# Two edits to a three-stage attention and MLP kernel: where a transposition is done, and how weights come back for a second batch

## The chip, the cores and the metric

The kernel runs on one core of a Trainium2 chip. A core has TensorE (PE in the profile; its weight loads are PEld), VectorE (DVE), ScalarE (ACT), GpSimd (POOL) and SyncE (SP), which here issues the DMAs; 16 DMA engines move the data. The metric is the device time of one execution in microseconds. Before the change the median of 3 runs is 804.38 us (803.98 to 806.12).

## The reference

Inputs are q, k and v, each 2 batches x 8 heads x 768 positions x 64, a 64 x 6 projection, and two pairs of weights, 512 x 2048 and 2048 x 512, in double precision.

```
bits   = (q @ proj > 0), (k @ proj > 0)           # 6 bits -> a bucket for each position
mask   = bucket(q) == bucket(k)
scores = where(mask, q @ k.T / 8, -1e9)
attn   = softmax(scores);  a = attn @ v           # 2 x 8 heads
x      = a, heads side by side                    # 1536 x 512
y      = relu(x @ w1_in)**2 @ w1_out              # first layer
h      = y @ w2_in
out    = max(0.01*h, h) @ w2_out                  # second layer, 1536 x 512
```

## The kernel before

Numbers are kept as a high and a low part, so that each product is three matmuls: high x high, low x high, high x low (function `three`).

**Attention.** A batch has four head pairs (`NPAIR`), and each pair 12 slots (`SLOTS`): a slot is one head and 128 query positions, 48 slots a batch (`N_ATT`). `prep` scales and splits q, k and v of a pair, transposes them and works out the bits. `slot` then does for one slot: four score matmuls (L633) into one bank of PSUM; VectorE's maximum, which also brings the scores to SBUF (L653, L657); ScalarE's exponential (L662); and the transposition of the 128 x 768 weights of the softmax, which must be had in two half-precision parts. That goes one of two ways. By DMA: ScalarE rounds to the high part (L691), GpSimd subtracts for the low part (L695), and one DMA transposes both (L709). By TensorE: six 128 x 128 transpositions into PSUM (L673), and ScalarE and VectorE read them out as high and low part (L681, L684). The product with v follows (L730 to L732, 18 matmuls), and after three slots the division (L754 to L759). In the first batch every second slot goes by TensorE (`BY_PE = 2`), and most of the others share one DMA for three slots (`group_of`, `SINGLE`). In the second batch all 48 go by DMA, one by one.

**MLP.** Each layer and batch has four groups (`group`). A group has an `up` half of 96 matmuls (4 blocks of 128 hidden units x 2 halves of the positions) and a `down` half of 96, or 72 wider ones in the second layer. After each `up` block come ACT L918, DVE L922, ACT L925 and POOL L930; after each `down` block DVE L964 adds to the sum. Between layers L973 to L976 split the sums again.

**Weights.** A group needs 8 tiles, 4 of w_in and 4 of w_out. In `weights`, a double-precision tile of 512 KB is fetched into one of three `wide` buffers (L840, L845), VectorE makes single precision of it in three integer passes (L855, L859, L862) into one of four `w32` buffers, ScalarE rounds to the high part (L871), and GpSimd subtracts for the low part (L876). A step that names two engines can also run on the second one; L876 does on VectorE 14 times. For the first layer the converted tile is also written to DRAM (L867, 256 KB), and for the second batch read back from there (L832) instead of being fetched and converted.

**Order.** Nothing is placed by hand. Each step is handed to `Plan` with the buffers it reads and writes, a due time and its engines with costs; `Plan.order` fixes one order per engine, and the engines then run in that order and wait on semaphores. The table of numbers (`SINGLE` to `HALVE`, `PITCH` to `COLD`) sets the due times. The steps come in this sequence: first batch's attention; first layer of the first batch, between whose matmuls the second batch's attention is laid; first layer of the second batch; second layer of both batches.

## Time and profile before

| | |
|---|---|
| median of 3 runs | 804.38 us |
| profiled execution, its own time | 808.95 us |
| its span, first to last instruction | 807.1 us |
| TensorE busy, of the span | 723.3 us, 90% |
| VectorE | 545.1 us, 68% |
| ScalarE | 412.4 us, 51% |
| GpSimd | 379.2 us, 47% |
| mean granted TensorE clock | 0.96 of full speed |

The span divides in three. Until 174 us only the first attention runs. From 174 to 412 us the first layer of the first batch and the second attention run together. From 412 us on there is only MLP: the rest of the first layer until about 541 us, then the second layer. "Busy" is the time in which an engine executes something; matmuls are pipelined, and a busy TensorE isn't necessarily one at its full rate. "DMA" is the mean busy share of the 16 DMA engines.

### The profile page before, as it was taken

The page shows a single profiled execution, that of the slowest core. Times are in us where ns is not written, and L with a number is a line of the kernel's source. Part 1 is how long each engine was busy: PE and PEld are TensorE (multiplying, and loading weights), DVE is VectorE, ACT ScalarE, POOL GpSimd, SP SyncE. Part 2 cuts the span into 40 slices and gives each one's busy share as a digit, 9 for nine tenths or more (in the row PEclk, how much of TensorE's full clock was granted, in tenths as well). Part 3 has the DMA queues.
Part 4 walks back from the last instruction along what each step waited for, and adds up shares of the span by engine and source line. Part 5 has one row for each costly group of instructions (what it writes and reads, how often), then busy time and mean ns, then how long its engine had stood idle before and what let it go on. Part 6 is the DMA issues. An engine that isn't in the chain of part 4 may idle for free.

```text
span 807.1 us, 14256 instructions
## 1 busy us (share of the span) xinstructions
PE 723.3 (90%) x5514; PEld 650.0 (81%) x5514; DVE 545.1 (68%) x1062; ACT 412.4 (51%) x681; POOL 379.2 (47%) x300
## 2 busy tenths in 40 slices
PE   4676758679999796997999999999999999999998
PEld 3464646568988694887999999999989899899896
DVE  7989899979998889996850232898164473655222
ACT  4777677758668566466653422544334034042230
POOL 3323133326668577477463644735256164163220
PEclk9989789879999998998999999999999999999999
DMA  3576767799999999999631323142130302300102
GB/s 118 108 177 130 176 119 167 143 230 217 235 217 180 238 228 224 224 219 188 120 86 53 92 79 106 53 131 81 50 105 1 105 27 78 105 27 1 45 35 78
DMA packets 185860, 100.81 MB, mean 125 GB/s; under 512 B 149440, under 2 KB 171968, under 8 KB 185792
## 3 DMA queue, kind: packets, MB, share of 16 engines
q1 hardware_dynamic: 185792, 99.90, 52.1%
q8 instruction: 43, 0.70, 0.4%
q14 instruction: 25, 0.20, 0.1%
HBM read 51.38 MB, written 11.53 MB: 78 GB/s over the span
## 4 chain that ended last, share of the span: by engine, by line
PE 69%; DVE 18%; issue 4%; DMA 4%; POOL 3%; ACT 2%; SPq 0%; DVEq 0%; POOLq 0%; ACTq 0%
PE acc L882 20%; PE acc L884 20%; PE acc L883 20%; DVE ep L653 3%; PE s L633 3%; DMA pt<-ep 3%; POOL ep L695 2%; PE av L730 1%; PE sx L673 1%; DVE pt L653 1%; PE av L732 1%; PE av L731 1%; DVE sm L657 1%; DVE w L862 1%; DVE s L466 1%
## 5 line engine op out<-in xcount | busy, mean ns | idle before, releaser
L930 POOL TENSOR_TENSOR g<-gx,g 128x384 fp32r<-128x384 f32 x126 | 134.9, 1088 | 142.7 <-ACT g L925 142.6
L882 PE MATMUL acc<-xh,wi 128*128 128x384 f32 x512 | 175.6, 343 | 0.3 <-DVE gx L922 0.3
L884 PE MATMUL acc<-xh,wi 128*128 128x384 f32 x512 | 171.9, 336 | 0.0
L883 PE MATMUL acc<-xl,wi 128*128 128x384 f32 x512 | 171.7, 335 | 0.0
L922 DVE SCALAR_TENSOR_TENSOR gx<-acc,rt 128x384 f32<-128x384 f32 x128 | 70.6, 555 | 122.9 <-ACT rt L918 121.6
L918 ACT ACTIVATE rt<-acc 128x384 f32<-128x384 f32 x128 | 62.8, 491 | 151.9 <-PE acc L884 151.4
L695 POOL TENSOR_TENSOR ep<-ep 128x768 f16<-128x768 f32 x52 | 91.6, 1767 | 78.9 <-ACT ep L691 47.4
L882 PEld LDWEIGHTS acc<-xh,wi 128*128 128x128 f32 x512 | 96.2, 188 | 2.4 <-DVE gx L922 0.6
L876 POOL TENSOR_TENSOR wo<-w,wo 128x512 fp32r<-128x512 f32 x38 | 53.1, 1416 | 92.5 <-ACT wo L871 62.4
L883 PEld LDWEIGHTS acc<-xl,wi 128*128 128x128 f32 x512 | 96.3, 188 | 0.3
L884 PEld LDWEIGHTS acc<-xh,wi 128*128 128x128 f32 x512 | 96.2, 188 | 0.0
L882 PE MATMUL acc<-g,wo 128*128 128x384 f32 x256 | 90.2, 352 | 0.0
L884 PE MATMUL acc<-g,wo 128*128 128x384 f32 x256 | 87.0, 340 | 2.9 <-DVE wo L876 2.9
L883 PE MATMUL acc<-g,wo 128*128 128x384 f32 x256 | 87.0, 340 | 0.0
L662 ACT ACTIVATE ep<-ep,sm,scs 128x768 f32<-128x768 f32 x60 | 61.6, 1027 | 37.8 <-DVE sm L657 35.4
L876 POOL TENSOR_TENSOR wi<-w,wi 128x512 fp32r<-128x512 f32 x44 | 64.5, 1472 | 34.0 <-ACT wi L871 34.0
L633 PE MATMUL s<-t 128*128 128x384 f16 x288 | 63.3, 345 | 15.2 <-DVE sm L657 15.2
L925 ACT CAST g<-gx 128x384 fp32r<-128x384 f32 x128 | 64.8, 509 | 19.9 <-DVE gx L922 19.7
L884 PE MATMUL acc<-wo,g 128*128 128x512 f32 x192 | 74.8, 390 | 0.0
L883 PE MATMUL acc<-wo,g 128*128 128x512 f32 x192 | 74.8, 390 | 0.0
L882 PE MATMUL acc<-wo,g 128*128 128x512 f32 x192 | 74.7, 389 | 0.0
L964 DVE TENSOR_TENSOR part<-acc,part 128x384 f32<-128x384 f32 (+1 forms) x66 | 38.8, 591 | 49.8 <-PE acc L884 49.5
(169 smaller groups left out, 1566.4 us busy)
## 6 DMA issues: line engine op xcount, KB each, us to landing
wide<-in_moe_w_in_dram SPq DMA_DIRECT2D x32, 512.0 KB, 4.7
w<-w SPq DMA_DIRECT2D x64, 256.0 KB, 3.2
wide<-in_moe_w_out_dram SPq DMA_DIRECT2D x32, 512.0 KB, 4.4
rawq<-in_q_dram SPq DMA_DIRECT2D x8, 384.0 KB, 3.4
rawk<-in_k_dram SPq DMA_DIRECT2D x8, 384.0 KB, 3.7
rawv<-in_v_dram SPq DMA_DIRECT2D x8, 384.0 KB, 3.9
out_dram<-part SPq DMA_DIRECT2D x6, 256.0 KB, 2.0
out_dram<-ep SPq DMA_DIRECT2D x6, 256.0 KB, 2.0
```

The costliest lines, as they stand in the source:

```text
L633: nc.tensor.matmul(out=ps[:, j, :HALF], lhsT=t[x][:, 0, n, :], rhs=t[x][:, 1, h * NTB + j * HB:h * NTB + (j + 1) * HB, :].rearrange("p n c ...
L662: do(d + EXP_AT, [smk, ("scs", x3)] + early, ek, act=(0.94, lambda: nc.scalar.activation(out=e, in_=e, func=ACTF.Exp, scale=scs[x3][:, 0:1 ...
L695: pool=(1.65, lambda: nc.gpsimd.tensor_tensor(out=p[:, 1, :], in0=e, in1=p[:, 0, :], op=ALU.subtract)),
L876: eng.tensor_tensor(out=lo, in0=o, in1=hi.bitcast(FP32), op=ALU.subtract)
L882: nc.tensor.matmul(out=acc, lhsT=st[0], rhs=mv[0], start=first, stop=False)
L883: nc.tensor.matmul(out=acc, lhsT=st[0], rhs=mv[1], start=False, stop=False)
L884: nc.tensor.matmul(out=acc, lhsT=st[1], rhs=mv[0], start=False, stop=last)
L918: do(d, [key], [rk], act=(0.37, lambda: nc.scalar.activation(out=rt, in_=bank()[:, :HALF], func=ACTF.Relu if L == 0 else ACTF.Copy)))
L922: do(d + 0.4, [key, rk], [gk], dve=(0.47, lambda: nc.vector.scalar_tensor_tensor(out=gx, in0=bank()[:, :HALF], scalar=scalar, in1=rt, op0= ...
L925: do(d + 1.1, [gk, "given"], [("g", r, j, 0)], act=(0.42, lambda: nc.scalar.copy(out=g_of(r, j)[0], in_=gx)), dve=(Port(0.27), lambda: nc. ...
L930: eng.tensor_tensor(out=gl, in0=gx, in1=gh.bitcast(FP32), op=ALU.subtract)
L964: do(d, [key] + yk, yk, dve=(0.07 + n * 0.00104, lambda: nc.vector.tensor_tensor(out=yp, in0=bank()[:, :n], in1=yp, op=ALU.add)))
```

## The change

The second batch no longer reads the first layer's converted weights from DRAM. It fetches all 32 double-precision tiles again and converts them again, and nothing is written to DRAM on the way. In the second attention every third slot is transposed by TensorE, in two halves of three blocks through the bank `t`, with a copy by ScalarE and a subtraction by VectorE for each half. In the first attention a fourth instead of half of the slots goes by TensorE, and the DMA transpositions are issued for one slot each (`SINGLE = 47` is more than there are). The scale of v has its own key (`scv`), and in the first pair it is worked out apart from that of q and k. `low` may also run on GpSimd, the half-precision identity is made by ScalarE, the projection is loaded from ScalarE's queue, and one memset is shortened. All numbers of the table are others.

```
-    SINGLE = 5
-    BY_PE = 2
-    MARGIN = 1.74
+    SINGLE = 47
+    BY_PE = 4
+    BY_PE1 = 3
+    MARGIN = 26.40
...
+        for cols, outs in (
+            ((slice(0, 2), [sc_k, ("pw", x2)]), (slice(2, 3), [scv_k]))
+            if by_head else ((slice(0, 3), [sc_k, scv_k, ("pw", x2)]),)
+        ):
+            level(a, p, s, cols, ...)
...
+    by_pe1 = [i for i in range(N_ATT) if i % BY_PE1 == BY_PE1 - 1]
...
         if b:
-            return place("ep", i % 2 * u, u), place("ep", (2 + i % 2) * u, u), place("pt", i % 4 * u, u)
+            half = None if i in by_pe1 else place("ep", (2 + i % 2) * u, u)
+            return place("ep", i % 2 * u, u), half, place("pt", i % 4 * u, u)
...
+        if half is None and b:
+            def turn_half(a):
+                for n in range(HB):
+                    c = (a * HB + n) * 128
+                    nc.tensor.transpose(psum["t"][0][:, n * 128:(n + 1) * 128], e[:, c:c + 128], ident)
+            for a in range(2):
+                hk, lk = ptk[a:a + 2], ptk[3 + a:5 + a]
+                do(d + TURN1_AT + a, ek, tb, pe=(0.33 * cold, lambda a=a: turn_half(a)))
+                do(d + TURN1_AT + a + 0.5, tb, hk, act=(
+                    0.37, lambda a=a: nc.scalar.copy(out=to[:, 0, a], in_=psum["t"][0][:, :HALF])
+                ))
+                do(d + TURN1_AT + a + 1, tb + hk, lk, dve=(0.47, lambda a=a: nc.vector.tensor_tensor(
+                    out=to[:, 1, a], in0=psum["t"][0][:, :HALF], in1=to[:, 0, a], op=ALU.subtract
+                )))
+            return
...
-            if L == 0:
-                do(d - KEEP, [ok], [kept], dma=(1.0, lambda: nc.sync.dma_start(out=where, in_=o)))
...
-        do(-7.5, [], [("pj_raw", hf)], dma=(0.05, lambda hf=hf: nc.sync.dma_start(
+        do(-20.0, [], [("pj_raw", hf)], dma=(0.05, lambda hf=hf: nc.scalar.dma_start(
...
-        nc.vector.tensor_copy(out=ident16, in_=ident)
+        nc.scalar.copy(out=ident16, in_=ident)
...
-            d = group(1, 0, g, d, 1.0, "kept")
+            d = group(1, 0, g, d, 1.0, "given")
```

Counted over each engine's whole order, VectorE has 32 more of each conversion pass, 32 subtractions from the bank `t`, 12 fewer of L684 and 14 fewer of L876; ScalarE has 32 copies from `t` and 12 fewer of L681; GpSimd has 14 more of L876 and 3 fewer of L695; TensorE has 96 transpositions more in the second attention and 72 fewer in the first; SP issues 64 fewer DMAs for `w32`, 32 more for `wide`, and 68 instead of 60 transpositions of softmax weights (36 and 32, where there were 12 and 48).

The order of SP in the first attention, before, from the first transposition of softmax weights (`part<-ep`, 36 blocks are three slots; `t<-s` is that of q and k):

```order
L709 DMA_TRANSPOSE part<-ep 128x36x128
L358 DMA rawv<-in_v_dram 128x2x384
L709 DMA_TRANSPOSE lg<-pt 128x36x128
L840 DMA wide_113<-in_moe_w_in_dram 128x4x256
L840 DMA wide_114<-in_moe_w_in_dram 128x4x256
L840 DMA wide_115<-in_moe_w_in_dram 128x4x256
L709 DMA_TRANSPOSE lg<-lo 128x36x128
```

The same place in the changed kernel (L748 is the transposition, L361 the load, L499 that of q and k, L879 the fetch):

```order
L748 DMA_TRANSPOSE part<-ep 128x12x128 x2
L361 DMA rawq<-in_q_dram 128x2x384
L499 DMA_TRANSPOSE t_82<-s_78 128x24x128
L748 DMA_TRANSPOSE part<-ep 128x12x128
L748 DMA_TRANSPOSE lg<-pt 128x12x128 x3
L361 DMA rawk<-in_k_dram 128x2x384
L748 DMA_TRANSPOSE lg<-lo 128x12x128 x3
```

Each slot has a DMA of its own now, and loads stand between the DMAs of one group.

The order of VectorE in the second group of the second batch's first layer, before (`gx` is L922, `part` is L964):

```order
L922 SCALAR_TENSOR_TENSOR gx_122<-acc_2215,rt_120 128x384
L922 SCALAR_TENSOR_TENSOR gx_123<-acc_2216,rt_121 128x384
L922 SCALAR_TENSOR_TENSOR gx_122<-acc_2217,rt_120 128x384
L922 SCALAR_TENSOR_TENSOR gx_123<-acc_2218,rt_121 128x384
L964 TENSOR_TENSOR part<-acc_2215,part 128x384
L964 TENSOR_TENSOR part<-acc_2216,part 128x384
```

The same group in the changed kernel (L894, L898 and L901 are the three passes of a conversion, L959 is `gx`, L1001 is `part`):

```order
L959 SCALAR_TENSOR_TENSOR gx_122<-acc_2171,rt_120 128x384
L959 SCALAR_TENSOR_TENSOR gx_123<-acc_2172,rt_121 128x384
L898 SCALAR_TENSOR_TENSOR w_118<-wide_115,w_118 128x512
L1001 TENSOR_TENSOR part<-acc_2169,part 128x384
L901 SCALAR_TENSOR_TENSOR w_118<-wide_115,w_118 128x512
L1001 TENSOR_TENSOR part<-acc_2170,part 128x384
L894 TENSOR_SCALAR w_119<-wide_113 128x512
L1001 TENSOR_TENSOR part<-acc_2171,part 128x384
L898 SCALAR_TENSOR_TENSOR w_119<-wide_113,w_119 128x512
L1001 TENSOR_TENSOR part<-acc_2172,part 128x384
L901 SCALAR_TENSOR_TENSOR w_119<-wide_113,w_119 128x512
```

Between the reads of TensorE's banks there now stand conversion passes, each waiting for a `wide` tile and a free `w32` buffer.

The end of the second attention on VectorE in the changed kernel, after the last maximum (L700 is the subtraction from the bank `t`, L825 and L1013 split the MLP's input, L793 to L798 are the division):

```order
L901 SCALAR_TENSOR_TENSOR w_118<-wide_115,w_118 128x512
L825 TENSOR_TENSOR xl_4426<-s_146,xh_4425 128x384
L700 TENSOR_TENSOR pt<-t_142,pt 128x384
L1001 TENSOR_TENSOR part<-acc_2171,part 128x384
L1013 TENSOR_TENSOR xl_106<-part,xh_105 128x384
L700 TENSOR_TENSOR pt<-t_142,pt 128x384
L825 TENSOR_TENSOR xl_4426<-s_146,xh_4425 128x384
L894 TENSOR_SCALAR w_119<-wide_113 128x512
L1001 TENSOR_TENSOR part<-acc_2172,part 128x384
L898 SCALAR_TENSOR_TENSOR w_119<-wide_113,w_119 128x512
```

The last subtractions for the attention stand among a conversion, the last sums of the first batch and the splits.

## Rows read from the trace of the kernel before

**Rows 1.** The page's 40 slices of the span, in tenths: three engines and the DMAs.

```profile
PE   4676758679999796997999999999999999999998
DVE  7989899979998889996850232898164473655222
DMA  3576767799999999999631323142130302300102
```

**Rows 2.** Busy time of each engine in stretches; columns are in the first line.

```profile
core 0: us, PE busy (x) PEld busy (x) DVE busy (x) ACT busy (x) POOL busy (x), PEclk, DMA share, GB/s
8.00:160.00 152.00, 106.85 (x1373) 82.02 (x1372) 138.74 (x342) 113.08 (x150) 48.77 (x38) 0.88 0.65 141
160.00:174.00 14.00, 8.69 (x87) 6.37 (x87) 11.80 (x25) 5.69 (x9) 0.00 (x0) 0.55 0.97 279
174.00:412.00 238.00, 215.70 (x1970) 193.01 (x1970) 208.04 (x409) 157.59 (x246) 158.81 (x109) 0.96 0.96 205
412.00:505.00 93.00, 93.00 (x552) 92.97 (x549) 24.52 (x44) 35.04 (x74) 45.63 (x41) 1.00 0.24 74
505.00:555.00 50.00, 50.00 (x291) 50.00 (x290) 42.33 (x58) 23.24 (x48) 30.30 (x23) 1.00 0.27 85
555.00:803.00 248.00, 248.00 (x1254) 225.36 (x1252) 114.08 (x169) 74.65 (x151) 92.03 (x80) 1.00 0.17 57
```

**Rows 3.** Chain of waits, 174 to 412 us: shares by line, and a long piece.

```profile
by line: PE acc L882 12.2%; PE acc L884 11.9%; PE acc L883 11.8%; DMA pt<-ep 8.9%; issue 8.8%; PE s L633 6.7%; DVE ep L653 6.3%; POOL ep L695 6.1%; DVE w L862 2.6%; ACT ep L691 2.4%; PE av L730 2.1%; DVE w L859 2.0%; PE av L732 2.0%; PE av 
...
360.47 6.36 DMA pt<-ep
```

**Rows 4.** DMA view, 174 to 412 us: the queue's packets, MB and share; two issues.

```profile
q1 hardware_dynamic: 111482, 48.50, 95.9%
...
w<-w SPq DMA_DIRECT2D x37, 256.0 KB, 3.6
...
pt<-ep SPq DMA_TRANSPOSE x48, 4.3
```

**Rows 5.** Groups of VectorE, 0 to 174 us: busy, mean ns, idle before.

```profile
L684 DVE TENSOR_TENSOR lo<-sx,lo 128x768 f16<-128x768 f32 x8 | 7.6, 949 | 0.1
...
L859 DVE SCALAR_TENSOR_TENSOR w<-wide,w 128x512 int32<-128x512 int32 x8 | 6.3, 800 | 0.0
```

**Rows 6.** Chain of waits at the end of the first attention: start, us, what.

```profile
154.35 1.65 POOL pt L695
156.01 4.86 DMA lg<-pt
```

**Rows 7.** SP's queue in order of time: one DMA of three slots, three of one.

```profile
35.70 6.01 SPq L709 DMA_TRANSPOSE part<-ep  x1
...
148.88 8.40 SPq L709 DMA_TRANSPOSE lg<-pt  x3
```

**Rows 8.** Groups of VectorE, 174 to 412 us.

```profile
L862 DVE SCALAR_TENSOR_TENSOR w<-wide,w 128x512 int32<-128x512 int32 x24 | 24.8, 1037 | 0.2
L859 DVE SCALAR_TENSOR_TENSOR w<-wide,w 128x512 int32<-128x512 int32 x24 | 22.5, 939 | 0.2
L855 DVE TENSOR_SCALAR w<-wide 128x512 int32<-128x512 int32 x24 | 19.9, 834 | 0.1
...
L876 DVE TENSOR_TENSOR wi<-w,wi 128x512 fp32r<-128x512 f32 x4 | 6.6, 1658 | 2.0 <-ACT wi L871 2.0
```

**Rows 9.** Groups by form over the whole span: a subtraction that reads PSUM.

```profile
L786 DVE TENSOR_TENSOR xl<-t,xh 128x384 fp32r<-128x384 f32 x10 | 5.5, 548 | 0.4 <-ACT xh L785 0.4
```

**Rows 10.** Chain of waits, 170 to 178 us: three transpositions of 128 x 128.

```profile
176.21 0.33 PE s L776 x3
```

**Rows 11.** Groups of VectorE, 505 to 555 us.

```profile
L859 DVE SCALAR_TENSOR_TENSOR w<-wide,w 128x512 int32<-128x512 int32 x8 | 7.7, 966 | 0.0
L862 DVE SCALAR_TENSOR_TENSOR w<-wide,w 128x512 int32<-128x512 int32 x8 | 7.6, 945 | 0.0
...
L855 DVE TENSOR_SCALAR w<-wide 128x512 int32<-128x512 int32 x8 | 6.5, 810 | 0.0
```

More of the change, by code (lines that the diff above doesn't have):

```diff
@@ L214, in lsh_attention_moe_moe_kernel @@
     KB = 1024
-    SINGLE = 5
+    SINGLE = 47
     BEHIND = 4
-    BY_PE = 2
-    PE_LAG = 6.72
-    SECOND = -1.33
-    VLATE = 1.28
-    OWN = 0.30
-    MARGIN = 1.74
-    MAX_AT = 3.72
-    EXP_AT = -0.48
-    HI_AT = 3.02
-    LO_AT = -5.50
-    TURN_AT = -21.75
-    DONE_AT = -8.05
-    PREP_AT = -1.23
-    PREP_STEP = 0.20
-    LAG0 = 0.08
-    FETCH = 10.12
-    CONVERT = 13.46
-    KEEP = -11.14
-    AGAIN = 29.85
-    FETCH0 = 1.46
-    LEAD0 = 64.75
-    CONVERT0 = -5.68
-    LOAD1_AT = -14.88
-    HALVE = 18.28
+    BY_PE = 4
+    BY_PE1 = 3
+    PE_LAG = 3.75
+    TURN1_AT = 1.00
+    SECOND = -13.33
+    PJ_AT = -7.00
+    VLEVEL = 0.42
+    VLATE = 1.11
+    OWN = 0.30
+    MARGIN = 26.40
+    MAX_AT = 2.58
+    EXP_AT = -2.20
+    HI_AT = 12.75
+    LO_AT = -23.34
+    TURN_AT = -10.62
+    DONE_AT = -18.25
+    PREP_AT = 0.03
+    PREP_STEP = 0.20
+    LAG0 = -2.87
+    FETCH = 15.82
+    CONVERT = 9.97
+    KEEP = -6.46
+    AGAIN = 19.38
+    FETCH0 = 3.80
+    LEAD0 = 47.11
+    CONVERT0 = 7.12
+    LOAD1_AT = -38.78
+    HALVE = 7.31
     const = ctx.enter_context(tc.tile_pool(name="const", bufs=1))
@@ L363, in rows, with level @@
         return raw[nm].rearrange("p h t d -> p (h t) d")
[L365 removed]
+    def level(t, p, s, cols, floors, targets, keys, outs, due):
         x = ring("level", 3)
+        n = cols.stop - cols.start
         row, dg, rk = lrow[x], ldiag[x], ("lrow", x)
         tb = [("tb", 0), ("tb", 1)]
[L372 removed]
+        do(due, keys, tb, pe=(0.1, lambda: nc.tensor.transpose(psum["t"][0][:n, 0:128], t[:, cols], ident)))
         do(due, tb, [rk], dve=(0.2, lambda: nc.vector.tensor_reduce(
@@ L430, in prep @@
             size(i, am_k[i], due(0) + i)
-        level(a, p, s, 3, floors, targets, am_k, [sc_k, ("pw", x2)], due(0) + 2)
+        for cols, outs in (
+            ((slice(0, 2), [sc_k, ("pw", x2)]), (slice(2, 3), [scv_k]))
+            if by_head else ((slice(0, 3), [sc_k, scv_k, ("pw", x2)]),)
+        ):
+            level(
+                a, p, s, cols, floors[:, cols], targets[:, cols], am_k[cols], outs,
+                due(0) + 2 + VLEVEL * (cols.start > 0),
+            )
         def scales():
@@ L764, in finished @@
         do(
-            d + DONE_AT, [("av", half, y) for y in range(HB)] + [("sc", x3)], [("x", hh, tq // HB), ("rd", half)],
+            d + DONE_AT, [("av", half, y) for y in range(HB)] + [("scv", x3)], [("x", hh, tq // HB), ("rd", half)],
             dve=(0.75, finish),
@@ L1002, in group @@
         return d
-    PITCH = 1.87
-    LEAD = 25.65
-    START = 11.26
-    MLP_OFF = 12.71
+    PITCH = 1.76
+    LEAD = 153.45
+    START = 4.17
+    MLP_OFF = 13.06
     MLP_AT = START + N_ATT * PITCH + MLP_OFF
     STRETCH = 1.87
-    AT1_OFF = -1.70
+    AT1_OFF = -15.95
     AT1 = MLP_AT + AT1_OFF
-    PITCH1 = 4.80
-    PREP1_AT = -6.56
-    PREP1_STEP = 5.71
+    PITCH1 = 5.03
+    PREP1_AT = -23.05
+    PREP1_STEP = 6.57
     COLD = 1.05
     for hf in range(2):
-        do(-7.5, [], [("pj_raw", hf)], dma=(0.05, lambda hf=hf: nc.sync.dma_start(
+        do(-20.0, [], [("pj_raw", hf)], dma=(0.05, lambda hf=hf: nc.scalar.dma_start(
             out=pj_raw[hf * D:(hf + 1) * D, :], in_=proj
@@ L1047, in lsh_attention_moe_moe_kernel @@
     )))
-    level(pam, ppw, psc, 1, pjlim[:, 0:1], pjlim[:, 1:2], ["pam"], ["psc"], -7.0)
+    level(pam, ppw, psc, slice(0, 1), pjlim[:, 0:1], pjlim[:, 1:2], ["pam"], ["psc"], PJ_AT)
     chain(
-        6.0, ["psc"], ["pp"],
+        PJ_AT + 1, ["psc"], ["pp"],
         (0.13, lambda: nc.vector.tensor_scalar(
```

28 lines of the change are left out of this document (15 added, 13 removed).

## The prediction

> **What bounds the kernel now.** The 40 slices [rows 1] come first, because one share for the whole span hides that there are stages. For nine slices VectorE is at 7 to 9 tenths and TensorE at 4 to 9. Then both stand near 9 and the DMAs at 9 too. From slice 21 on TensorE is full and everything else has room. The table of stretches [rows 2] puts numbers on it.
>
> *Stage one*, to 174 us: VectorE is busy 138.74 of the 152 us between 8 and 160, 91%; TensorE has 70%, ScalarE 74%, GpSimd 32%, the DMAs 65%. So VectorE sets the pace. Only in the last 14 us is it something else: the last transpositions by DMA, which show as a GpSimd piece of 1.65 us and a DMA of 4.86 us right behind each other [rows 6].
>
> *Stage two*, 174 to 412 us: three things are nearly full together. VectorE is busy 208.04 of 238 us (87%), TensorE 215.70, and the DMA queue holds the engines for 95.9% of the time [rows 2, 4]. The chain of waits says what ends last when TensorE stops: transpositions by DMA 8.9%, "issue" 8.8%, GpSimd's subtraction ahead of them 6.1%, VectorE's maximum 6.3% [rows 3]. The last piece shown there is a transposition that took 6.36 us, against a median of 4.3 from issue to landing. Some 24% of 238 us, 57 us, of the path thus lies on the way of a slot through GpSimd and the DMAs.
>
> *Stage three*, from 412 us: TensorE is busy every microsecond, and at its rate: 552 matmuls in 93 us is 0.168 us each. Only more work for TensorE, or a wait that doesn't exist yet, can make it longer.
>
> **Stage one, after.** VectorE loses 12 subtractions of 0.949 us [rows 5], 11.4 us. It loses the cast of the identity, and gains the second, one-column scale of v, some seven small instructions; I let these two cancel. A stage that runs at 91% of VectorE then shrinks by 11.4/0.91 = 12.5 us. GpSimd gets 12 more subtractions at 1.65 us [rows 6], 20 us, and has 103 us to spare in the 152 [rows 2]; ScalarE exchanges 12 copies from PSUM for 12 roundings of nearly one length. TensorE loses 72 transpositions, which were beside VectorE's work. SP's queue is the one that gets fuller: three single DMAs hold it 8.40 us, one DMA of three slots 6.01 [rows 7], so 36 at 2.8 us are 101 us where there were six of 6.0 and six of 2.8, 53 us. With 36 slots the queue is taken for about two thirds of the stage, and a slot no longer waits for two others, so I cost this at nothing; if loads of q, k or v are late behind it, it is the cover that has gone. The tail of 14 us stays: the last slot but one still goes by GpSimd and DMA. Bounds: nothing is gained if the chain of one slot and not VectorE paces the stage (0), all of VectorE's idle time there goes too (12.5 + 13.3, about 26); I take 13, the row of the pace. Stage one: 174 to 161 us.
>
> **Stage two, after: what goes.** The DMAs lose 16 slots (0.39 MB each, 6.3 MB) and all 37 transfers of `w32` in this stage (9.7 MB [rows 4]), and get some 10 fetches of 0.52 MB more, since 32 instead of 24 tiles are converted there and the next are under way: 5.2 MB. That is 10.8 MB less of 48.5. At the stage's own rate, 228 us for 48.5 MB, it is 51 us less: 177 of 238, no longer a bound. GpSimd loses 15 subtractions (25 us at 1.65).
>
> **What comes.** TensorE: 32 times three transpositions at 0.33 us [rows 10], 10.6 us, all in a stage where it has 22 us of slack. VectorE: 32 subtractions from PSUM at 0.548 [rows 9], 17.5 us; 8 conversions (24 becomes 32) at 0.834 + 0.939 + 1.037 = 2.81 [rows 8], 22.5 us. It loses seven of L876, which the order leaves to GpSimd now, between 1.2 and 1.66 us [rows 8], some 10 us; and about 11 us of splits of x, casts and second choices that move behind the stage or to ScalarE and GpSimd. Sum 17.5 + 22.5 - 21 = 19: VectorE goes from 208 to 227 us. A pass of L859 takes 0.800 us in stage one, where GpSimd is busy 32%, and 0.939 in stage two, where it is busy 67% [rows 2, 5, 8]; with GpSimd at about 60% the 32 conversions get back some 4 us: 223.
>
> So the bound passes from the DMAs to VectorE. With 223 us of work the stage is between 226 us (the 98% that would be a queue that never waits) and 245 us (the 91% of stage one). I take 236 us, between the two, because more of its queue is conversions, which can be done while a slot is waited for. The new wait is at the bank `t`: the second half of a slot's transposition needs ScalarE's copy and VectorE's subtraction of the first, and behind it in TensorE's order stand the score matmuls of the next slot. Where VectorE is late by a conversion, it costs up to 2.8 us each time; it is inside the span of 226 to 245. Stage two: 238 to 236 us.
>
> **Stage three, after.** The order has 30 matmuls of the second batch's first group ahead of the last slot's product before, and those stand behind it now: 30 x 0.168 = 5.0 us, with 9 more transpositions of x 6 us. Then the 24 conversions that were reads from DRAM: 8 in each of three groups, with 8 more for the second layer's first group as before. What such a group costs can be seen already: between 505 and 555 us VectorE does eight conversions of 0.810 + 0.966 + 0.945 = 2.72 us and is busy 42.33 of 50 us, while TensorE is busy 50.00 of 50 [rows 2, 11]. In a group of 32 us (192 matmuls) eight conversions are 21.8 us and sixteen readings of TensorE's banks at 0.55 are 8.8: 30.6, or 95%, tighter than that window. I add 3 us of waits. If no wait comes it is 0; if VectorE's queue sets the pace at 91%, each of four groups takes 33.6 instead of 32 us and the split of x at the end comes on top, 12 us in all. Stage three: 391 to 400 us.
>
> **Sum.** 161 + 236 + 400 = 797 us against 803, and the last 4 us stay: 801 us of span, 6 less than 807.1. The profiled execution's own time was 808.95, which is 4.6 over the median of the runs; on the median, 804.4 - 6 = 798 us. A difference of 0.3%, 2.4 us, is what a measurement of this kernel can tell from no change.
>
> **Rivals.**
>
> *The DMAs were the bound, and nothing takes their place.* For it speak the 95.9% and the 57 us of the path on that way. Then VectorE's queue closes up to 98% (226 us), stage three needs no wait (397), and stage one ends three us earlier for the shorter start: 158 + 226 + 397 + 4 = 785 us of span, 781 on the median. Against it: VectorE was at 87% and gets 19 us more.
>
> *VectorE becomes the pace from 161 us to the second layer.* This ends on the other side. Its place is the second attention and the four groups behind it, its price the 91% at which VectorE ran when it did set the pace: 245 in stage two, 409 in stage three (6 + 12). With stage one at 162 it is 820 us of span, 817 on the median. It decides from the point where stage two's VectorE work, 223 us, takes over 242 us. For it speaks that in every third slot TensorE waits for two readings of `t` by VectorE, and that conversions stretch beside GpSimd. The Trainium skill, "GPSIMD Engine Reference", section "1. Specifications", has a rule for this: GpSimd's SBUF interfaces are shared with VectorE, and the contention is with VectorE instructions that have two SBUF inputs or run in a two-port mode. By that rule the conversions would suffer wherever GpSimd is at work, and the subtractions from PSUM would not; the trace agrees as far as it goes, with 0.800 against 0.939 us for L859. Against it: the 505 to 555 us window, where 85% did not hold TensorE up.
>
> *Stage one doesn't shrink.* If a slot's chain and SP's fuller queue pace it, it loses 3 us, and with the other terms as forecast the span is 171 + 236 + 400 + 4 = 811 us, 808 on the median.
>
> **How the numbers follow.** The forecast has 0.46, its own range 788 to 807 (stage two 228 to 243, stage one 158 to 164). The first rival has 0.21, the second 0.21, the third 0.12. Of the forecast three quarters are under 802 us and the rest about half each within and above the bound; with all of the first rival, faster is 0.35 + 0.21 = 0.56. Within 0.3% are 0.06 of the forecast and 0.06 of the third case: 0.12. The rest, 0.32, is slower. The range of 8 in 10 reaches from 781, the first rival's time, to 815, a little short of the second's.
>
> **What would show it.** VectorE's share over the stage before the first MLP matmul should stay near 91% with that matmul near 161 us; the DMAs' share of stage two should fall to about 75%; the chain there should name VectorE where it named the transpositions. TensorE should be busy throughout after the attention, with conversions of about 2.7 us. I am wrong if TensorE waits on VectorE in the four groups behind the attention, if the DMAs' share stays over 90% (then it wasn't bytes that filled them), or if the first MLP matmul doesn't move.

## The result: 816.0 us, 1.4% slower, and the profile after

The changed kernel takes 815.96 us (median of 4 runs, 813.92 to 818.73) against 804.18 for the kernel before on the same chip: a ratio of 1.014 (95% interval 1.011 to 1.018). Its profiled execution took 817.97 us, with a span of 816.2. The 40 slices, TensorE, VectorE and the DMAs:

```profile
PE   2776666689989899899699999999999999999998
DVE  5888889978788899899989798899367367554222
DMA  2599988986965876866524343342222103100112
```

Against [rows 1] the DMAs have changed places: the row of nines in stage two has gone to 5 to 8, and nines stand now in stage one. The stretches, in the columns of [rows 2]:

```profile
0.00:23.00 23.00, 7.86 (x73) 5.75 (x74) 12.79 (x60) 9.63 (x17) 4.06 (x21) 1.00 0.31 103
23.00:160.00 137.00, 93.72 (x1240) 69.48 (x1238) 119.65 (x294) 109.09 (x143) 64.53 (x40) 0.88 0.87 174
160.00:172.00 12.00, 7.49 (x88) 5.86 (x86) 10.96 (x25) 4.08 (x7) 0.94 (x1) 0.50 1.11 228
172.00:415.00 243.00, 225.39 (x2028) 202.07 (x2026) 210.84 (x437) 156.51 (x255) 140.35 (x99) 0.94 0.71 158
415.00:548.00 133.00, 133.00 (x781) 132.85 (x778) 118.44 (x161) 56.28 (x114) 81.35 (x61) 1.00 0.37 116
548.00:812.00 264.00, 264.00 (x1347) 241.38 (x1345) 139.25 (x187) 83.29 (x169) 112.50 (x92) 1.00 0.19 61
```

The first MLP matmul, by which stage one ends, in the list of TensorE in order of time:

```profile
172.37 0.67 PE L919 MATMUL acc<-xh,wi 128*128 128x384 f32 x1
```

It was forecast for 161. The chain of waits in stage two [rows 3], then the DMA view there [rows 4]:

```profile
by line: PE acc L919 15.4%; PE acc L920 14.7%; PE acc L921 14.7%; PE s L652 12.0%; DVE ep L672 7.7%; PE av L769 3.9%; PE t L692 3.2%; PE av L771 3.2%; DVE w L898 3.1%; PE av L770 3.1%; issue 2.6%; DVE w L901 2.0%; DVE pt L700 1.7%; DVE xtok
```

```profile
q1 hardware_dynamic: 84820, 38.15, 70.9%
...
pt<-ep SPq DMA_TRANSPOSE x32, 3.7
```

The transpositions and GpSimd's subtraction are no longer among the shares that the line shows, and "issue" fell from 8.8% to 2.6%; the score matmuls (L652) and VectorE's maximum (L672) have the larger shares now. Cut at the same three events (first MLP matmul, last product with v, last matmul), the span moves like this:

| us | before | after | difference | forecast |
|---|---|---|---|---|
| stage one, to the first MLP matmul | 174.4 | 172.4 | -2.0 | -13 |
| stage two, to the last product with v | 237.9 | 242.7 | +4.8 | -2 |
| stage three, to the last matmul | 390.7 | 396.9 | +6.2 | +9 |
| end | 4.1 | 4.2 | +0.1 | 0 |

Between the two profiles the span grows by 9.1 us, between the medians the time grows by 11.8: the profiled execution lay 4.8 us above the median before and 2.0 us above it after.

### The profile page after: what moved, and what is told of

Same layout as the page of the kernel before. It is cut to its first block, busy times and chain, and to the rows that moved or that the text cites. A ratio compares the mean times of both kernels' runs of the same rounds, so it can differ in the third digit from the quotient of the medians.

```text
span 816.2 us, 14398 instructions
## 1 busy us (share of the span) xinstructions
PE 731.8 (90%) x5540; PEld 657.4 (81%) x5540; DVE 612.6 (75%) x1162; ACT 418.9 (51%) x702; POOL 403.7 (49%) x313
## 4 chain that ended last, share of the span: by engine, by line
PE 74%; DVE 16%; DMA 3%; issue 3%; ACT 2%; POOL 1%; DVEq 0%; POOLq 0%
PE acc L919 21%; PE acc L921 21%; PE acc L920 21%; PE s L652 4%; DVE ep L672 3%; DMA t<-s 2%; DVE w L898 2%; PE av L769 1%; PE av L771 1%; PE av L770 1%; DMA part<-ep 1%; PE t L692 1%; DVE sm L676 1%; POOL ep L734 1%; DVE s L478 1%
## 5 line engine op out<-in xcount | busy, mean ns | idle before, releaser
L967 POOL TENSOR_TENSOR g<-gx,g 128x384 fp32r<-128x384 f32 x128 | 148.0, 1171 | 123.6 <-ACT g L962 122.0
L959 DVE SCALAR_TENSOR_TENSOR gx<-acc,rt 128x384 f32<-128x384 f32 x128 | 69.9, 551 | 73.4 <-ACT rt L955 72.6
L913 POOL TENSOR_TENSOR wo<-w,wo 128x512 fp32r<-128x512 f32 x48 | 66.7, 1401 | 94.2 <-ACT wo L908 94.2
L898 DVE SCALAR_TENSOR_TENSOR w<-wide,w 128x512 int32<-128x512 int32 x96 | 103.2, 1080 | 0.4
L734 POOL TENSOR_TENSOR ep<-ep 128x768 f16<-128x768 f32 x36 | 65.0, 1809 | 71.5 <-ACT ep L730 44.8
L919 PEld LDWEIGHTS acc<-xh,wi 128*128 128x128 f32 x512 | 97.5, 190 | 1.9 <-DVE gx L959 0.8
L921 PEld LDWEIGHTS acc<-xh,wi 128*128 128x128 f32 x512 | 97.3, 190 | 0.0
L913 POOL TENSOR_TENSOR wi<-w,wi 128x512 fp32r<-128x512 f32 x48 | 69.3, 1447 | 50.8 <-ACT wi L908 47.2
L901 DVE SCALAR_TENSOR_TENSOR w<-wide,w 128x512 int32<-128x512 int32 x96 | 93.9, 983 | 0.3
L894 DVE TENSOR_SCALAR w<-wide 128x512 int32<-128x512 int32 x96 | 71.6, 754 | 11.0 <-POOL wo L913 8.8
L681 ACT ACTIVATE ep<-ep,sm,scs 128x768 f32<-128x768 f32 x60 | 61.7, 1028 | 35.3 <-DVE sm L676 30.7
L921 PE MATMUL acc<-wo,g 128*128 128x512 f32 x192 | 74.8, 390 | 0.0
L920 PE MATMUL acc<-wo,g 128*128 128x512 f32 x192 | 74.8, 390 | 0.0
```

The lines of the kernel that those rows point to most:

```text
L734: pool=(1.65, lambda: nc.gpsimd.tensor_tensor(out=p[:, 1, :], in0=e, in1=p[:, 0, :], op=ALU.subtract)),
L894: (Port(0.34), lambda: nc.vector.tensor_scalar(out=oi, in0=t[:, :, 1], scalar1=3, scalar2=0x3FFFFFF8, op0=ALU.logical_shift_left, op1=ALU. ...
L898: (Port(0.6), lambda: nc.vector.scalar_tensor_tensor(out=oi, in0=t[:, :, 0], scalar=29, in1=oi, op0=ALU.logical_shift_right, op1=ALU.bitwi ...
L901: (Port(0.6), lambda: nc.vector.scalar_tensor_tensor(out=oi, in0=t[:, :, 1], scalar=-0x40000000, in1=oi, op0=ALU.bitwise_and, op1=ALU.bitw ...
L913: eng.tensor_tensor(out=lo, in0=o, in1=hi.bitcast(FP32), op=ALU.subtract)
L919: nc.tensor.matmul(out=acc, lhsT=st[0], rhs=mv[0], start=first, stop=False)
```

## The experiments

Edits that change a due time or a step make the planner lay out the whole program anew. So there are two kinds of kernels here. Those named e (but for e1) are planned anew; those named p, and e1, keep the changed kernel's order, instruction by instruction, but for the one edit. Ratios are to the kernel before, run on the same chip; the times are those of the profiled execution, cut as above.

| kernel | ratio (95%) | stage one | two | three |
|---|---|---|---|---|
| changed | 1.014 (1.011 to 1.018) | 172.4 | 242.7 | 396.9 |
| e0 nudged | 1.017 (1.016 to 1.019) | 169.5 | 246.7 | 397.5 |
| e1 projection later | 1.012 (1.009 to 1.015) | 172.0 | 243.0 | 396.8 |
| e2 every 2nd slot by TensorE | 1.022 (1.020 to 1.025) | 171.9 | 248.9 | 397.5 |
| e9 every 3rd | 1.032 (1.029 to 1.036) | 174.1 | 259.3 | 395.9 |
| e3 three slots a DMA | 1.017 (1.014 to 1.020) | 180.2 | 237.9 | 397.9 |
| e4 no halves by TensorE | 1.019 (1.017 to 1.022) | 173.0 | 238.9 | 403.6 |
| e5 weights kept in DRAM | 1.015 (1.012 to 1.018) | 172.7 | 243.8 | 396.8 |
| e6 before, refetched | 1.021 (1.018 to 1.025) | 170.4 | 238.9 | 407.3 |
| e7 before, halves by TensorE | 1.013 (1.010 to 1.016) | 171.7 | 241.5 | 396.7 |
| p1 half the DMA bytes | 1.010 (1.008 to 1.011) | 169.7 | 240.8 | 396.8 |
| p5 VectorE +11 us, stage one | 1.022 (1.019 to 1.026) | 181.6 | 238.0 | 396.9 |
| p6 VectorE -11 us, stage one | 1.009 (1.007 to 1.012) | 169.7 | 242.8 | 396.8 |
| p7 no GpSimd, half the bytes | 0.990 (0.987 to 0.994) | 158.6 | 241.7 | 396.8 |
| p8 no GpSimd, twice the DMAs | 1.020 (1.017 to 1.023) | 178.6 | 241.5 | 396.9 |
| p9 GpSimd +59 us | 1.041 (1.038 to 1.044) | 196.8 | 243.1 | 396.8 |
| p2 TensorE +10.5 us, stage two | 1.014 (1.012 to 1.015) | 173.0 | 242.3 | 396.8 |
| p3 VectorE +20 us, stage two | 1.034 (1.033 to 1.036) | 173.0 | 253.1 | 402.6 |
| p4 VectorE -25 us, stage two | 1.003 (1.001 to 1.005) | 169.8 | 237.7 | 396.8 |

**How small a difference says something.** e0 is `PITCH = 1.77` for 1.76.

> The changed kernel with one due time of the first attention nudged (1.77 instead of 1.76 a slot), so that the order is planned anew with no other edit: a control for what a new order alone does. All theories: within 5 us of 816; what it differs by is the size below which an edit that replans says nothing.

A new order alone moved stage one by -2.9 and stage two by +4.0 us. It can do more: e2 and e9 below edit nothing of stage two, and theirs is 6.2 and 16.6 us longer. And in the four profiles in which stage one is the same to the last instruction (changed, p2, p3, p4) it ends between 169.8 and 173.0. I read nothing from less than 4 us of a stage where the order is kept, and of the kernels planned anew I take a stage's length as a hint only.

### Stage one: where the 11 us of VectorE went

My first theory after the result was the queue of single transpositions: the DMA share of stage one had risen from 0.65 to 0.87, and in the chain of 62 to 96 us "DMA t<-s" and "DMA part<-ep" had 42%. The rival was the start. The chain of the first 26 us (start, us, what):

```profile
1.93 4.38 DMA pj_raw<-in_proj_dram
...
9.64 0.85 DVE am L422
```

The projection's steps wait for their load and stand ahead of k's size (L422), so the first score matmul comes at 22.7 instead of 18.4 us. e1 puts these steps behind the first scale:

```
-        for n, e, _ in plan.order():
-            plan.steps[n][2][e][1]()
+        for n, e, _ in plan.order():
+            if pj_first <= n < pj_last: late.append((n, e)); continue
+            plan.steps[n][2][e][1]()
+            if ("sc", 0) in plan.writes[n]: ...   # the late steps follow here
```

> The changed kernel with its order kept, but the steps on the projection (its largest value, its scale, its parts) stand behind the first scale of q and k on VectorE, TensorE and GpSimd instead of ahead of them. Theory 'queue' (the body of stage one is held by SP's queue of single transpositions): the first score matmul comes at about 19 to 20 us instead of 22.7, but the third head pair still starts near 95 us, the first MLP matmul stays at 170 to 173 us, and the time is 0 to 1.5 us under the changed kernel's 816. Rival 'head' (the late start is the loss): first MLP matmul near 168 us and 812 us or less.

First score 21.5, first MLP matmul 172.0. The edit gave back only 1.2 of the 4.3 us of the start, less than expected, and 0.4 of it showed at the end. What the other 3.1 us cost was not tried: the start is not ruled out as a part of the loss. For the queue, p1 moves half the bytes and nothing else:

```
-    out=t_all.rearrange("p (n c) -> p n c", c=128), in_=p_all
+    out=t_all.rearrange("p (n c) -> p n c", c=128)[:, :(2 if b else 1) * NTB],
+    in_=p_all[:, :(2 if b else 1) * S],
...
-    out=o, lhsT=pt[:, NTB + kb, :], ...
+    out=o, lhsT=pt[:, low + kb, :], ...      # low = 0 for these slots
```

> The changed kernel in its own order; each of the 36 DMA transpositions of the first attention moves only the high part of the softmax weights, half the bytes, and the product with v of these slots takes the high part again in place of the low one. Nothing else changes on any engine. Theory 'queue': between 23 and 160 us the DMAs' share falls from 0.87 to about 0.65, the third head pair starts before 90 us instead of at 95, the first MLP matmul comes at 160 to 166 us, the time at 804 to 810 us. Rival 'chain' (the steps between the engines, not the DMAs, hold the pairs): third pair at 93 us or later, first MLP matmul at 170 us or later, the time within 3 us of 816.

The DMA share between 23 and 160 us fell to 0.64, as expected, and the first MLP matmul came at 169.7, inside the spread. The queue's bytes alone are not the pace: my theory fell, as far as it was one of bytes. e2 and e9 change `BY_PE` (4 to 2, 4 to 3), e3 `SINGLE` (47 to 5):

> The changed kernel with every second slot of the first attention transposed by TensorE (as before the change) instead of every fourth; the rest of the table stays, the order is planned anew. Theory 'queue': 24 instead of 36 DMA transpositions, each 2.3 to 2.8 us of SP's queue, so the DMAs' share between 23 and 160 us falls from 0.87 to about 0.7 and the first MLP matmul comes at 165 us or earlier, the time at 805 to 811 us. Rival 'VectorE paces stage one' (the prediction's own reason): 12 more subtractions of 0.95 us, the first MLP matmul at 180 us or later, the time 822 us or more.

> The changed kernel with every third slot of the first attention transposed by TensorE instead of every fourth; the order is planned anew. Between the two ends tried (every fourth: DMAs 0.87, VectorE 87%; every second: DMAs 0.74, VectorE 95%; both end stage one at 172 us). Theory 'steps between engines': first MLP matmul within 3 us of 172, the time within 5 us of 816. Rival 'two bounds that cross': 165 us or earlier and 809 us or less.

> The changed kernel with one DMA for three slots again in the first attention (but for the last five); the order is planned anew. All theories by now: the DMAs don't hold stage one, so the first MLP matmul stays within 4 us of 172 and the time within 5 us of 816 to 820. If the queue of single transpositions did count: 166 us or earlier.

In e2, with 12 subtractions more, VectorE was busy 130.72 of 137 us (95%), the DMAs fell to 0.74, and stage one ended at 171.9, between its two theories: two different mixes, one time. e9 kept stage one near 172, but its stage two, which the edit doesn't touch, is 16.6 us longer; I read nothing more from it. e3 was 8 us later in stage one, which neither of its theories had. That waiting for two other slots costs more than it spares the queue would fit; it isn't shown. Then VectorE, both ways. p5 does the subtraction twice, p6 leaves two passes of the first eight conversions out:

```
-    dve=(0.87, lambda: nc.vector.tensor_tensor(out=to[:, 1], in0=..., in1=to[:, 0], op=ALU.subtract))
+    dve=(0.87, lambda: [nc.vector.tensor_tensor(out=to[:, 1], ...) for _ in range(2)])     # p5
...
-    (Port(0.6), lambda: nc.vector.scalar_tensor_tensor(
+    (Port(0.6), lambda: first or nc.vector.scalar_tensor_tensor(      # p6, two passes
```

> The changed kernel in its own order; each of the 12 subtractions that read TensorE's bank in the first attention is done twice: 12 x 0.95 = 11.4 us more of VectorE in stage one, as much as the change took out. Theory 'steps between engines' (VectorE, 87% busy, waits in stage one for the prepared pair and not the other way round): the first MLP matmul moves by less than 4 us from 172.4. Rival 'VectorE paces stage one' (the prediction's reason): it moves by 9 to 13 us, to 181 or later.

> The changed kernel in its own order; the second and third integer pass of the first eight conversions, all in the first attention, are left out (the weights of these tiles are wrong): 8 x (1.06 + 0.83) = 15 us less of VectorE in stage one. Theory 'VectorE paces stage one, on both sides': the first MLP matmul at 160 to 164 us. Rival 'only the edge' (VectorE at 87% waits more when it has less to do; the slots' chain takes over): 167 us or later, about 4 us earlier than 172 at most, and the time within 5 us of 816.

Adding 11.4 us made stage one 9.2 us longer, as the rival "VectorE paces stage one" had it; taking 11.3 us out (130.68 to 119.41) made it 2.7 shorter, inside the spread. From the first score to the first MLP matmul, the changed kernel and then p6:

```profile
22.70:172.40 149.70, 101.91 (x1338) 75.89 (x1336) 130.68 (x318) 113.47 (x152) 65.46 (x40) 0.85 0.89 178
```

```profile
22.70:169.70 147.00, 101.82 (x1338) 75.40 (x1338) 119.41 (x302) 112.98 (x152) 65.32 (x40) 0.85 0.91 181
```

VectorE goes from 87% to 81%: it waits. For whom, p7 and p9 tell: GpSimd's subtraction in the first attention left out, with half the bytes, or done twice.

```
-    pool=(1.65, lambda: nc.gpsimd.tensor_tensor(out=p[:, 1, :], in0=e, in1=p[:, 0, :], op=ALU.subtract))
+    pool=(1.65, lambda: b and nc.gpsimd.tensor_tensor(...))                           # p7, p8
+    pool=(1.65, lambda: [nc.gpsimd.tensor_tensor(...) for _ in range(1 if b else 2)]) # p9
```

> The changed kernel in its own order; in the first attention the 36 slots that go by DMA have no low part: GpSimd's 36 subtractions of 1.65 us are left out, each DMA transposition moves only the high part, and the product takes the high part twice. Theory 'the slot's chain through GpSimd and the DMA paces stage one': first MLP matmul at 163 us or earlier. Rival 'VectorE's queue of small steps between the engines': 168 us or later, as with the halved DMAs alone (169.7).

> The changed kernel in its own order; each of GpSimd's 36 subtractions in the first attention is done twice: 36 x 1.65 = 59 us more of GpSimd, from 47% to about 85%, and 1.65 us more in the chain of each of these slots. Theory 'slot's chain': the first MLP matmul comes 10 us later or more, 182 us or later. Rival 'GpSimd has room' (the prediction's reason for costing it at nothing): less than 4 us later.

The two, from the first score to the first MLP matmul, p7 and then p9:

```profile
22.70:158.60 135.90, 95.39 (x1336) 70.76 (x1336) 119.01 (x318) 112.55 (x152) 5.29 (x4) 0.90 0.70 143
```

```profile
22.70:196.80 174.10, 109.59 (x1336) 79.53 (x1332) 149.09 (x318) 114.44 (x151) 133.22 (x76) 0.80 0.77 153
```

With GpSimd out and half the bytes, stage one ends at 158.6, 13.8 us earlier, though VectorE has as many instructions (x318) as in the changed kernel. With GpSimd's work doubled, it ends 24.4 us later. So the step isn't free, though GpSimd is only 64.53 of 137 us busy in the changed kernel.

Neither edit leaves VectorE as it was, though. Its instructions take 119.01 us in p7, 130.68 in the changed kernel and 149.09 in p9; some of them take longer the more GpSimd does (the last section has their times). In p9 that is 18.4 us more of VectorE. p5 paid 9.2 us for 11.9 more, so some 14 of p9's 24.4 us, an estimate from these two runs, can have come through VectorE. p9 alone doesn't tell that road from the slot's chain. In p7 VectorE has 11.7 us less, and by p6 as much less of VectorE gains 2.7 us at most.

What tells GpSimd's step from the bytes is p1 against p7: both move half the bytes, and they differ in the 36 subtractions alone. p1, from the first score to the first MLP matmul:

```profile
22.70:169.70 147.00, 100.00 (x1337) 74.96 (x1338) 132.65 (x318) 113.37 (x152) 65.43 (x40) 0.86 0.66 135
```

With the subtraction it takes 147.00 us, without it 135.90: 11.1 us go with GpSimd's step. VectorE's busy time falls by 13.6 us along with it, and these runs don't divide the 11.1 us between that and the step's own place in the chain. For the place speaks that VectorE's relief alone gained 2.7 us at most (p6): the step's 1.65 us and the DMA behind it stand in the chain of 36 slots instead of 24. (p7 is the one kernel here that beats the kernel before, by 1.0%, but with softmax weights of one half-precision part: it is a measurement, not a replacement.) p8 should have shown the same at full bytes: no subtraction, and the high part transposed by two DMAs of six blocks.

> The changed kernel in its own order; in the first attention GpSimd's 36 subtractions are left out, and the DMA transposes the high part twice (two DMAs of six blocks, the second into the low part's place), so that as many bytes move as in the changed kernel. Theory 'GpSimd's step in the slot's chain paces stage one': first MLP matmul at 165 us or earlier with the DMAs' share still 0.85 or more. Rival 'only both together': 168 us or later.

It came out late, at 178.6, as the rival had it:

```profile
22.70:178.60 155.90, 102.20 (x1336) 75.80 (x1333) 120.02 (x318) 112.94 (x151) 5.07 (x4) 0.85 0.89 170
```

VectorE and GpSimd have about as little to do as in p7, and the bytes are those of the changed kernel, in 72 DMAs instead of 36; it ends 6.2 us later than the changed kernel, and 20.0 later than p7 with half of the DMAs and half of the bytes. So less work on both engines gains nothing while each slot waits for two DMAs. That the number of DMAs counts, where p1's bytes did not, is the likely reading. What GpSimd's step costs at the full bytes of the changed kernel stays open.

### Stage two: TensorE's work and its clock

p2 does the 96 transpositions twice (`for n in [*range(HB)] * 2`), p3 the first conversion pass twice from the ninth tile on (`for _ in range(1 if first else 2)`), p4 leaves the third pass out there (`lambda: first and ...`).

> The changed kernel in its own order; TensorE does each of the 96 transpositions of the second attention twice into the same place. Theory 'TensorE's work shows in full': stage two 242.7 plus 96 x 0.11 = 10.5, about 253 us, and 826 us in all. Rival 'slack' (TensorE waits in stage two for others, 10 us more lie inside its waits): stage two under 247 us, the time under 820 us.

> The changed kernel in its own order; the first integer pass of a conversion is done twice from the ninth tile on: 32 x 0.64 = 20 us more of VectorE in stage two (210.8 to about 231 of 243 us, 95%), some 20 us more in the four groups behind it. Theory 'VectorE is not the pace': stage two grows by less than 5 us, the four groups by less than 3, the time under 824 us. Rival 'VectorE is the pace of stage two': stage two grows by 12 to 20 us, the time 828 us or more.

> The changed kernel in its own order; the third integer pass of a conversion, which puts the sign in, is left out from the ninth tile on (the weights of these tiles lose their sign): 32 x 0.95 = 30 us less of VectorE in stage two, 210.8 to about 181 of 243 us. Theory 'VectorE paces stage two': half of it or more shows, as half of an addition did: stage two 242.7 to 230 or less, the time 804 us or less. Rival 'VectorE has only the edge' (adding hurts, taking away finds the next bound, TensorE's 225 us): stage two 236 us or more.

Stage two of p2, p3 and p4, from the first MLP matmul to the last product with v:

```profile
173.00:415.30 242.30, 227.33 (x2123) 206.48 (x2120) 212.15 (x437) 156.97 (x255) 140.75 (x99) 0.98 0.71 158
```

```profile
173.00:426.10 253.10, 225.26 (x2025) 200.43 (x2023) 230.49 (x469) 156.39 (x255) 139.09 (x99) 0.95 0.68 152
```

```profile
169.80:407.50 237.70, 221.47 (x2026) 198.25 (x2024) 185.34 (x406) 155.58 (x255) 136.28 (x99) 0.96 0.73 162
```

By its length p2 looks like its rival, slack: 10.5 us of work for nothing. But the granted clock stands at 0.98 there and at 0.94 in the changed kernel. The clock records show two levels, full and half. What the lower one takes from a stage is at most (1 - granted) x length; from the records that is 8.5 us before, 14.8 in the changed kernel and 4.8 in p2. Take it off, and p2's stage is 237.5 us against 228.0: 9.5 of 10.5 show. The check on this step is eight profiles in which nothing of stage two differs (changed, e1, p1, p5 to p9): 238.0 to 243.1 us long, and 228.0 to 229.8 without what the clock took. So TensorE's work does show, and what hid it in p2 was the clock, at full speed for more of the stage when TensorE had more to do between its waits. Its other runs agree: the mean clock of the whole span is 0.966 to 0.969 in the four of p2, and 0.954 to 0.960 in the four of the changed kernel. p3 is 241.6 without the clock, 13.6 of its 20 us. p4 is 229.3, nothing for its 25 us, as its rival had it. p4's time did fall all the same, to 1.003 of the kernel before against 1.014, clear of both intervals. In its profile stage two is 5.0 us shorter, and all of that is the clock's part: 8.4 us instead of 14.8. So VectorE at 87% is on the edge: more of it makes the stage longer, and less of it, in p4's profile, shortens the stage only by what the clock gives back.

### The parts of the change by themselves

e4 sets `BY_PE1 = 99`, e5 puts the write to DRAM and `"kept"` back, e6 and e7 make the second and the first of these parts on the kernel before.

> The changed kernel with no slot of the second attention transposed by TensorE (all 48 by DMA, as before); weights still fetched and converted again. Theory 'TensorE's work shows in full': stage two (first MLP matmul to last product with v) loses the 96 transpositions of 0.11 us, 242.7 to about 232 us, and the time comes to about 806 us; the DMAs, with 32 x 0.39 MB less relief, stand at 0.75 to 0.85 of the stage and do not bind. Rival 'the DMAs bound stage two and TensorE's halves relieved them': stage two 240 us or more, the time 814 us or more.

> The changed kernel, but the converted weights of the first layer are written to DRAM and read back for the second batch, as before; everything else as changed, the order planned anew. Theory 'refetching costs nothing': the 32 conversions of 2.7 to 2.95 us lie beside TensorE's work, so the time stays within 3 us of 816, with the DMAs of stage two up from 0.71 to 0.8 to 0.9. Rival 'conversions make VectorE the pace of stage two': stage two shrinks by 5 to 10 us and the time falls to 806 to 811 us.

> The kernel before with one part of the change: the first layer's weights are fetched and converted again for the second batch, nothing is written to DRAM; the order is planned anew. Theory 'refetching alone costs nothing': the DMAs of stage two fall from 0.96 to about 0.8, VectorE gets 8 conversions there, the time stays within 4 us of the kernel before. Rival 'DMAs were the bound': 8 us or more faster. Rival 'VectorE': 8 us or more slower.

> The kernel before with one part of the change: every third slot of the second attention transposed by TensorE in two halves; conversions kept in DRAM as before, the order planned anew. The DMAs of stage two fall from 0.96 to about 0.85. Theory 'relief and work cancel' (waits 7 us less, TensorE's work 10.5 us more, the clock either way by 6): within 8 us of the kernel before. Rival 'the DMAs were the bound': 8 us or more faster.

e5 agrees with its theory: with the changed table the refetching costs nothing that these runs can tell. On the kernel before (e6) it costs 2%, as its rival "VectorE" had it: stage three is 407.3 us, 16.6 more than before. Of that 39 matmuls that stand behind the cut now account for 6.6 us, and TensorE stands still in the groups behind the attention:

```profile
409.30:560.00 150.70, 145.65 (x833) 143.23 (x830) 134.94 (x190) 62.84 (x128) 80.38 (x61) 0.99 0.39 117
```

VectorE is at 90% there and TensorE idle for 5 us. What the other 5 us are is open. e4 missed on both theories: stage two has 12 us less of TensorE's work (the 96 transpositions, and 9 matmuls that moved behind the cut) and became only 3.8 us shorter, with the DMAs at 0.87, and stage three 6.7 longer, 1.5 of it for the 9 matmuls. e7 has the DMAs of stage two down from 0.96 to 0.77 and gained nothing: it is 1.0 to 1.6% slower, more than the 8 us expected. None of the parts, done or undone alone, beats the kernel before; with what a new order alone does to a stage (4 us in e0, 16.6 in e9), these runs don't give their sizes.

## Why the prediction was wrong, step by step

**Stage one, forecast -13, measured -2.0: the step that failed.** The first half of it held: VectorE is busy 12.4 us less before the first MLP matmul (155.8 to 143.4), for 11.4 forecast. What failed is "a stage that runs at 91% of VectorE then shrinks by 11.4/0.91", and with it that GpSimd's 12 subtractions have "103 us to spare" and that SP's fuller queue was costed "at nothing". The stage did not follow VectorE. Of the 12.4 us, 2.0 were gained; the rest became idle time of VectorE: 4.6 us in the first 22.7 us, where the projection's load is waited for (busy 12.7 us for 17.3), and 5.8 us between there and the first MLP matmul. Its share fell to 130.68 of 149.7 us, 87%. The stretches that this is read from, beside those above, before and then after:

```profile
0.00:18.40 18.40, 6.72 (x64) 5.24 (x65) 14.23 (x54) 8.24 (x13) 6.68 (x21) 1.00 0.40 127
18.40:22.70 4.30, 3.29 (x25) 1.75 (x23) 3.08 (x12) 3.88 (x7) 0.00 (x0) 1.00 0.02 6
18.40:174.40 156.00, 109.95 (x1412) 83.81 (x1410) 141.61 (x330) 113.68 (x151) 45.70 (x28) 0.85 0.69 155
```

```profile
0.00:18.40 18.40, 4.13 (x36) 2.75 (x36) 9.37 (x47) 5.92 (x10) 4.06 (x21) 1.00 0.31 104
18.40:22.70 4.30, 3.43 (x38) 2.84 (x36) 3.35 (x12) 3.42 (x7) 0.00 (x0) 1.00 0.34 108
```

The waits of VectorE after, from 20 to 165 us (who waits, for whom, us, times, longest):

```profile
DVE ep L672 <- PE sx L652: 2.7, 3, 1.0
DVE xb L548 <- PE t L536: 2.4, 3, 1.4
DVE part L723 <- ACT part L720: 2.4, 2, 2.2
DVE rd L793 <- PE av L771: 1.7, 3, 1.1
...
DVE pt L672 <- POOL ep L734: 1.1, 1, 1.1
```

All such waits sum to 14.8 us, where they were 9.1 before; they are spread over many steps, and the longest is 2.2 us. p6 and p7 say what they mean: with still less VectorE stage one moves by no more than its spread, with half the bytes and no step on GpSimd in the slots' chain it does. The start was left out of the prediction's sum: the first score comes 4.3 us later, e1 gave 1.2 of that back, and what the rest costs is open. The rival "stage one doesn't shrink" had the mechanism, a slot's chain through GpSimd and SP's DMAs, and its -3 us; I gave it 0.12, because I weighed GpSimd by the room it has and not by its place in the chain.

**Stage two, forecast -2, measured +4.8.** The DMA term was right (0.71 for a forecast 0.75), and so were the chain's new names. VectorE's work was mis-sized: 210.84 us for 223. The conversions and subtractions, 172 to 415 us [rows 8, 9]:

```profile
L898 DVE SCALAR_TENSOR_TENSOR w<-wide,w 128x512 int32<-128x512 int32 x32 | 34.9, 1096 | 0.0
L901 DVE SCALAR_TENSOR_TENSOR w<-wide,w 128x512 int32<-128x512 int32 x31 | 29.3, 948 | 0.0
L894 DVE TENSOR_SCALAR w<-wide 128x512 int32<-128x512 int32 x32 | 20.4, 643 | 0.0
L700 DVE TENSOR_TENSOR pt<-t,pt 128x384 f16<-128x384 f32 x32 | 17.6, 549 | 1.7 <-ACT pt L698 1.7
```

The subtractions are as forecast (0.549); a conversion is 2.69 for 2.81 us, and more splits went elsewhere than I counted. Without the clock's part it didn't matter, as p4 shows. Two things failed. One is that TensorE's 10.6 us lie "in a stage where it has 22 us of slack": in p2, 9.5 of 10.5 such us show once the clock's part is off. The other is that the sum has no term for the clock. The matmuls before the cut fell from 807 to 777, so TensorE's net gain in work is 10.5 - 5.0 = 5.5 us; without the clock's part the stage went from 229.4 to 228.0, so its waits fell by 6.9, and the clock took 6.3 more. That is the +4.8, to the rounding. The -1.4 us without the clock is near the -2 forecast, but by two terms that nearly cancel, which the forecast didn't have: luck. The 6.3 us rest on one profile of each kernel. In the eight profiles of the unchanged stage the clock took 8.2 to 15.0 us, so how much of the 6.3 the change brought is open. Whether the 6.9 us came from the DMAs' relief is open too: e7 had the relief without them, in an order of its own. (Two slips in the working change nothing here: 223 us at 98% are 228 us and not 226, and the first rival's span of 785 us is 782 on the median and not 781.)

**Stage three, forecast +9, measured +6.2.** The moved work is all of it: 30 matmuls and 9 transpositions of x, 6.0. The 3 us of waits were not there; TensorE is busy 133.00 of 133 us beside conversions of 2.95 us, longer than the 2.72 forecast [rows 11]:

```profile
L901 DVE SCALAR_TENSOR_TENSOR w<-wide,w 128x512 int32<-128x512 int32 x30 | 33.4, 1115 | 0.1
L898 DVE SCALAR_TENSOR_TENSOR w<-wide,w 128x512 int32<-128x512 int32 x29 | 28.5, 985 | 0.2
L894 DVE TENSOR_SCALAR w<-wide 128x512 int32<-128x512 int32 x30 | 25.3, 849 | 0.3 <-DMA wide<-in_moe_w_out_dram 0.3
```

p3, with 20 us more there, is where such waits begin (402.6). The rival "VectorE becomes the pace" had the time, 817, by a road that was not taken: no group behind the attention was held up.

## What to carry to other kernels

A busy share says more about what a stage costs if work is added to that engine than about what it gains if work is taken away: in stage one, at 87%, adding 11 us to VectorE cost 9, and removing 11 gained less than could be measured. Something else then ends within a few us. Before work is moved to an engine with room, ask whether it stands in the chain that each tile runs through, and which instructions of its neighbours it makes longer: with half the bytes in both, leaving GpSimd's 1.65 us out of 36 such chains gained 11.1 us. And compare stages with the clock's part taken off, above all where an edit makes TensorE idle more or less between its waits.

## What the runs showed of the hardware that I had not expected

- **More matmuls, same time.** With 96 transpositions added to a stage with TensorE 93% busy, its granted clock stood at 0.98, where the eight profiles of the unchanged stage have 0.94 to 0.97, and the stage was 0.4 us shorter than the changed kernel's.
- **Conversions beside an idle GpSimd.** p7 has the changed kernel's order, but GpSimd does next to nothing in stage one. The passes of the eight conversions there, from 20 us to the first MLP matmul, in p7 (L900, L903 and L896 are L898, L901 and L894):

```profile
L900 DVE SCALAR_TENSOR_TENSOR w<-wide,w 128x512 int32<-128x512 int32 x8 | 5.8, 733 | 0.0
L903 DVE SCALAR_TENSOR_TENSOR w<-wide,w 128x512 int32<-128x512 int32 x8 | 5.7, 725 | 0.0
L896 DVE TENSOR_SCALAR w<-wide 128x512 int32<-128x512 int32 x8 | 3.2, 419 | 0.0
```

and in the changed kernel:

```profile
L898 DVE SCALAR_TENSOR_TENSOR w<-wide,w 128x512 int32<-128x512 int32 x8 | 8.4, 1058 | 0.0
L901 DVE SCALAR_TENSOR_TENSOR w<-wide,w 128x512 int32<-128x512 int32 x8 | 6.5, 828 | 0.0
L894 DVE TENSOR_SCALAR w<-wide 128x512 int32<-128x512 int32 x8 | 3.2, 418 | 0.0
```

The two passes with two inputs are 44% and 14% longer beside GpSimd's work; the pass with one input keeps its time here. It is GpSimd and not the DMAs: p1, with half the bytes and GpSimd at work, has 1058 and 830 ns, and p8, with the full bytes and no subtractions, 733 and 681. The subtraction from PSUM (L723) keeps 0.95 us in p7, the changed kernel and p9. That is the rule of contention that the prediction cited from the Trainium skill, "GPSIMD Engine Reference", section "1. Specifications", and here it has a size. In p9, with GpSimd's work doubled, the two passes take 798 and 876 ns, so the size isn't fixed: it depends on what lies beside them. Two things don't follow from the number of inputs. A half-precision copy with one input (L491, eight of 128x768) stretches most of all:

```profile
L491 DVE COPY s<-s 128x768 f16<-128x768 f16 x8 | 2.6, 352 | 0.0
```

in p7, and in the changed kernel:

```profile
L491 DVE COPY s<-s 128x768 f16<-128x768 f16 x8 | 5.5, 712 | 0.0
```

In p9 it takes 1311 ns. The rule's other case is a two-port mode; no run here shows whether this copy runs in one. And the conversion's pass with one input takes 643 and 849 ns in stages two and three (rows above); why is open.
- **Two half DMAs are no cheaper than one whole.** 72 transpositions of six blocks, with GpSimd's subtractions left out, made stage one 6.2 us longer than 36 of twelve blocks with them (p8 against the changed kernel); half the bytes in the same 36 (p1 against the changed kernel) saved 2.7 at most.
